# Attention by chunks with a gated MLP behind it: room for w_in from the start, ten pairs of buffers, and another order of the first batch's dense work

## The chip, the cores and the metric

The kernel runs on one core of a Trainium2 chip. The metric is the device time in microseconds of one execution. A core has five engines with a queue each: PE (matmul), DVE (vector), ACT (activation and copies), POOL (GpSimd) and SP, which here issues all DMAs. Each engine works through its queue in order, and an instruction that waits holds back everything behind it.

## The reference

```python
for t in range(S):                     # B, H, S, D = 4, 8, 768, 40
    y[:, :, t] = einsum('bhd,bhde->bhe', rt, state)
    Sa = einsum('bhde,bhe->bhd', state, at)
    state = state * wt - outer(Sa, bt) + outer(vt, kt)
x = y as (B, S, 320)
h = gelu(x @ w_in)                     # 320 x 1024, tanh form
u, v = halves of h
v_n = (v - mean) / sqrt(var + 1e-6) * g_ln
v_s = einsum('ts,bsd->btd', w_sg, v_n) + b_sg
out = x + (u * v_s) @ w_out            # 512 x 320
```

## The kernel before

The recurrence is worked in 12 chunks of 64 steps, for the four batches (b = 0 to 3) side by side. For each chunk there are gates (`gate_w` to `gate_k`, scans of the decays and products of keys, ahead of the chain by two to three chunks), the inverse of a triangular matrix (row steps on DVE, then the long list of steps on POOL that write `tg` and `x`, then `inv_back` with DVE transposes into `x1z` and `xt`, then `inv_g` and `inv_x` on PE) and the chain `chain1` to `chain5`, in which the state passes from chunk to chunk. `chain5` writes `yt`, and SP stores it to `xd`, the input of the dense part.

The order of all instructions is written out by hand: every step has a position in a plan, 28 positions to a chunk and 14 to a half chunk (c, hf), and `half` sorts the steps of a half by position. Each engine keeps this program order. Position 252 is the start of chunk 9, 336 that of the last half, in which only the y of the last chunk is left.

The dense part (`Mlp`) works in pairs of float32r numbers, a high half h and a low half l, that stand for one float32. `split64` brings one 128 x 256 tile of w_in (or a part of w_out) into such a pair in six steps: `load` (SP, into one of three buffers `stg`), `size` (ACT), `fields` and `scale` (DVE), `parts` (ACT), `low` (three steps on DVE or POOL). Twelve tiles make up w_in. `DEC` gives each tile's position and its engine for `low` (0 DVE, 1 POOL), and `DSTEP` the distance of the six steps from it. Before, `PIN` is 266.02, the position at which the gates' pool has been closed: only there `open_in` allots wih, wil, the stage buffers and the temporaries, so no tile is loaded earlier. `PX` loads half of the first batch's x (4 DMAs), `PS` splits it, `PL` loads the other half, and `PF` issues the three pieces v0, v1 and v2 while the attention part still runs.

The pieces are v0 to v5 (8 products of 512 columns, gelu, normalization, and the pair vh, vl), u0 to u7 (8 products of 384 columns, gelu), s0 to s7 (18 products with w_sg, then gate and the pair gy, gx) and o0 to o5 (products with w_out, add of x, store). s wants all six v of its batch. o0 to o2 want s0 to s3, o3 to o5 want s4 to s7. `product` issues a piece's products, and the steps behind it follow at once, one or two pieces later. `FIRSTS` is the order of the first pieces, `SEQ` that of one batch's s and o with the next batch's v and u between them. At places of this order stand the splits of w_sg (`SGS`, engine by `SGE`: V DVE, G POOL) and the six steps of the eight tiles of w_out (`OUTS`, `OSTEP`, `OUTE`).

Of the kernel before, what the change touches and what calls it, by code (L numbers as in the profile page):

```python
# [69 lines left out]
FILLERS = ("v0", "v1", "v2")  # L70
FIRSTS = ("v0", "v1", "v2", "u1", "u0", "u2", "v3", "u3", "v4", "v5", "u4", "u5", "u6", "u7")
SEQ = ("s1", "s2", "s0", "s3", "s4", "v0", "s5", "v1", "o0", "o1", "o2", "s6", "s7", "v2", "u0", "v3", "u1", "v4",
    "v5", "o3", "o5", "o4", "u2", "u3", "u4", "u5", "u7", "u6")
XS = 0
REST = 8
# [57 lines left out]
def attention(tc, a, xd, flag, keep, ps, mlp=None):  # L133
# [4 lines left out]
    with ExitStack() as ctx:  # L138
# [9 lines left out]
        ring_a, ring_a_end = pool("at_ring_a", "left")  # L148
        gt, gt_right = pool("at_gate", "right")
# [464 lines left out]
class Mlp:  # L614
# [3 lines left out]
    def __init__(self, tc, ps, xd, w_in, w2, g_ln, wst, b_sg, w_out, out):  # L618
        self.tc, self.ps, self.xd, self.out = tc, ps, xd, out
        self.w_in, self.w2, self.g_ln, self.wst, self.b_sg, self.w_out = w_in, w2, g_ln, wst, b_sg, w_out  # L620
        self.V, self.A, self.G, self.T, self.Q = engines(tc)
        self.ctx = ExitStack()
        self.vn, self.us, self.gs = {}, {}, {}
        self.n, self.todo, self.plan = 0, [], None
# [4 lines left out]
    def open_in(self):  # L629

        self.ps.grow()
        self.sb = p = self.pool("mlp_in", "right")
        self.wih, self.wil = (p.tile([128, 3, DF], F32R, name=n) for n in ("wih", "wil"))
        self.mhalf = p.tile([128, 1], F32, name="mhalf")
        self.G.memset(self.mhalf, -0.5)

    def open_x(self):
        p = self.pool("mlp_x", "right")
        self.xts = [p.tile([128, 3, S], F32, name=f"xt{i}") for i in range(2)]
        self.xh = p.tile([128, 3, S], F32R, name="xh")  # L640
        self.xl = p.tile([128, 2, S], F32R, name="xl")

    def open_v(self):
        self.pv = self.pool("mlp_v", "right")

    def open_rest(self):
        self.pr = p = self.pool("mlp_rest", "left")
        self.wsh, self.wsl = (p.tile([128, 6, S], F32R, name=n) for n in ("wsh", "wsl"))
        self.woh = p.tile([128, 4, DM + 64], F32R, name="woh")
        self.wol = p.tile([128, 4, DM - 64], F32R, name="wol")  # L650
        self.bt = p.tile([128, S], F32, name="bt")
        self.gl = p.tile([128, 4], F32, name="gl")

# [77 lines left out]
    def weights_rest(self):  # L731
        def part_sg(k, c):
            n = S // 2
# [22 lines left out]
        def rest():  # L756
            for t in (self.gl, self.bt):
                self.V.tensor_scalar(out=t, in0=t, scalar1=0.5, scalar2=None, op0=ALU.mult)
# [4 lines left out]
        wo = [part_out(k, c) for c in range(2) for k in range(4)]  # L763
        return [load_rest, rest], loads, parts, wo

    def load_x(self, b, n):

        Q, t = self.Q, self.xts[b % 2]
        c = slice(384 * n, 384 * n + 384)
        for k in range(2):  # L770
            Q.dma_start(out=t[:, k, c], in_=self.xd[b, 128 * k:128 * k + 128, c])
        for k in range(2):
            Q.dma_start(out=t[64 * k:64 * k + 64, 2, c], in_=self.xd[b, 256:320, c])

# [23 lines left out]
    def in_v(self, b, tt):  # L798
# [8 lines left out]
        bs = sb.tile([128, 6], F32, name="bs", bufs=3)  # L807

# [16 lines left out]
    def in_u(self, b, f, n):  # L825
# [5 lines left out]
        u = self.us[b, f, n] = self.pr.tile([128, 384], F32, name="u", bufs=8)  # L831
        self.product([(o, *x) for x in ops], *self.gelu2(o, 384, u))

    def sgu(self, b, f, n):
# [6 lines left out]
        o = self.ps("sg")[:, 0:384]  # L841
        g = sb.tile([128, 384], F32, name="g", bufs=2)

        def one():
            V.scalar_tensor_tensor(out=g, in0=o, scalar=self.gl[:, f:f + 1], in1=self.bt[:, c], op0=ALU.mult, op1=ALU.add)
            V.tensor_tensor(out=g, in0=g, in1=self.us.pop((b, f, n)), op=ALU.mult)
# [7 lines left out]
    def outp(self, b, m, n):  # L854
# [4 lines left out]
        o = self.ps("op")[:, 0:384]  # L859
        ops = []  # L860
# [9 lines left out]
        def one():  # L870
            x = self.xts[b % 2]
            y = sb.tile([128, 384], F32, name="y", bufs=2)[0:r]
            if m < 2:
                V.tensor_tensor(out=y, in0=o, in1=x[:, m, c], op=ALU.add)
            else:
                V.tensor_tensor(out=y, in0=o[64:128], in1=x[64:128, m, c], op=ALU.add)
# [5 lines left out]
    def side(self, c, hf):  # L882
# [5 lines left out]
        if self.plan is None:  # L888
            self.plan = plan
            at(PIN, self.open_in)  # L890
# [11 lines left out]
            at(PS, lambda: self.split_x(0, 0))  # L902
            at(PV, self.open_v)
            at(PL, lambda: self.load_x(0, 1))
            for k, p in enumerate(PF):
                at(p, lambda k=k: self.in_v(0, k))
# [3 lines left out]

    def run(self, ahead, verdict=None):

        if not ahead:
            self.open_in()
# [5 lines left out]
            for n in range(2):  # L920
                self.load_x(0, n)
            self.split_x(0, 0)
        self.open_rest()
        names = [x for x in FIRSTS if not ahead or x not in FILLERS]
        seq, jobs = [(x, 0) for x in names], [(XS, lambda: self.split_x(0, 1))]
        for b in range(B):
            if b + 1 < B:
                p = len(seq)
                for n in range(2):
                    jobs += [(p, lambda b=b, n=n: self.load_x(b + 1, n)), (p + 1, lambda b=b, n=n: self.split_x(b + 1, n))]  # L930
            seq += [(x, b + (x[0] in "uv")) for x in SEQ if x[0] in "so" or b + 1 < B]
            if b == 1 and verdict:
                jobs.append((p + 6, lambda: self.later((8, 9, verdict()))))
# [10 lines left out]
        for i, (x, b) in enumerate(seq):  # L944
            while jobs and jobs[0][0] <= i:
                jobs.pop(0)[1]()
            k = int(x[1])
            if x[0] == "u":
                self.in_u(b, k % 4, k // 4)
            elif x[0] == "v":  # L950
                self.in_v(b, k)
            elif x[0] == "s":
                self.sgu(b, k % 4, k // 4)
            else:
                self.outp(b, k % 3, k // 3)
# [114 lines left out]
```

## Time and profile before

| | us |
|---|---|
| median of 3 runs (lowest to highest) | 674.15 (673.51 to 678.35) |
| profiled execution, span from first to last instruction | 676.4 |
| PE busy | 582.4 |
| DVE busy | 525.3 |
| ACT busy | 391.3 |
| POOL busy | 367.2 |

The profiled execution's own time is not given beside its span; the span is 2.2 us above the median of the runs. Times in the rows are microseconds from the start of the span. A row of the timeline holds start, duration, engine, line, operation, target and sources with their shapes, count, and in brackets how long the engine stood idle ahead of it and for whom. PEclk 1.00 is 2.4 GHz, 0.50 is 1.2 GHz. All instructions have the same line because a helper records them, so they are told apart by their tiles.

### The profile page before, as it was taken

The numbers are of one execution on the slowest core, as the hardware profiler recorded it, in microseconds if no ns is written. First come the engines' busy times: TensorE is split into PE (matmuls) and PEld (weight loads), VectorE is DVE, ScalarE is ACT, GpSimd is POOL, SyncE is SP. The second block draws the span as 40 slices with busy tenths as digits, with TensorE's granted clock in tenths as the row PEclk, the third lists the DMA queues.
The fourth block names the chain that finished last, engine by engine and source line by source line (L and its number), as shares of the span: only waits on it lengthen the run. The fifth ranks groups of instructions, "written<-read, shape, count | busy, mean of one in ns | idle before, by whom it ended". The sixth has DMA issues, their size and how long they took to land.

```text
span 676.4 us, 22453 instructions
## 1 busy us (share of the span) xinstructions
PE 582.4 (86%) x8950; PEld 525.1 (78%) x8950; DVE 525.3 (78%) x1204; ACT 391.3 (58%) x1106; POOL 367.2 (54%) x813
## 2 busy tenths in 40 slices
PE   6336899989999899998978798697599999999996
PEld 5235787878888788887967687586599999999995
DVE  7898879889889898898777547888769668757742
ACT  5445767979779788797755644552345234434410
POOL 5216786877877878778781423544532334232321
PEclk9555589999999999999978678888699999999998
DMA  6731234343433443433334322340103001100001
GB/s 220 215 98 44 77 99 112 100 108 109 126 110 109 111 116 106 109 90 99 92 99 118 96 71 69 102 136 13 32 1 100 1 30 51 49 31 1 29 24 41
DMA packets 57617, 56.54 MB, mean 84 GB/s; under 512 B 35936, under 2 KB 47456, under 8 KB 57504
## 3 DMA queue, kind: packets, MB, share of 16 engines
q1 hardware_dynamic: 57504, 55.02, 28.4%
q8 instruction: 72, 1.18, 0.7%
q14 instruction: 41, 0.34, 0.2%
HBM read 47.14 MB, written 7.86 MB: 81 GB/s over the span
## 4 chain that ended last, share of the span: by engine, by line
PE 45%; DVE 25%; ACT 17%; issue 7%; DMA 3%; POOL 1%; SPq 1%; DVEq 0%; POOLq 0%; ACTq 0%
PE sg L119 12%; PE hu L119 7%; PE hv L119 6%; PE op L119 6%; PE ab L119 4%; ACT xt L119 3%; DVE sc L119 3%; PE sp L119 3%; DVE x L119 2%; PE pq L119 2%; DVE at L119 2%; ACT nts L119 2%; PE ru L119 2%; ACT gs L119 2%; PE yp L119 2%
## 5 line engine op out<-in xcount | busy, mean ns | idle before, releaser
L119 POOL TENSOR_TENSOR tg<-x,n 128x126 f32<-128x126 f32 (+21 forms) x318 | 116.9, 368 | 51.7 <-DVE x L119 14.2
L119 POOL TENSOR_TENSOR x<-x,tg 128x126 f32<-128x126 f32 (+21 forms) x318 | 122.2, 384 | 24.9
L119 POOL TENSOR_TENSOR gx<-g,gy 128x384 fp32r<-128x384 f32 x32 | 33.0, 1034 | 89.7 <-ACT gy L119 89.7
L119 PE MATMUL sg<-wsh,vh 128*128 128x384 f32 x192 | 66.9, 349 | 5.4 <-ACT vh L119 5.0
L119 PE MATMUL ab<-at,kb 64*64 64x64 f32 x1536 | 44.5, 246 | 29.9 <-POOL kb L119 14.2
L119 ACT ACTIVATE nts<-ab 32x256 f32<-32x256 f32 x192 | 62.2, 324 | 13.6 <-DVE at L119 11.2
L119 PE MATMUL sg<-wsh,vl 128*128 128x384 f32 x192 | 66.7, 348 | 1.5 <-POOL vl L119 1.5
L119 PE MATMUL sg<-wsl,vh 128*128 128x384 f32 x192 | 66.5, 346 | 0.7 <-POOL wsl L119 0.7
L119 PEld LDWEIGHTS ab<-at,kb 64*64 64x64 f32 x1536 | 35.2, 153 | 39.6 <-POOL kb L119 15.8
L119 PE MATMUL pq<-rt,vut 128*128 128x128 f32 x384 | 60.6, 306 | 3.4 <-ACT vut L119 2.9
L119 PEld LDWEIGHTS pq<-rt,vut 128*128 128x128 f32 x384 | 52.3, 211 | 6.6 <-ACT vut L119 3.1
L119 ACT CAST gy<-g 128x384 fp32r<-128x384 f32 x32 | 16.4, 513 | 70.6 <-DVE g L119 70.6
L119 PE MATMUL yp<-pqs,kbt 128*64 128x64 f32 x768 | 49.0, 233 | 4.2 <-DVE pqs L119 3.1
L119 ACT COPY vs<-sc 64x160 f32<-64x160 f32 x88 | 28.3, 321 | 37.0 <-DVE sc L119 36.1
L119 ACT CAST vh<-v 128x512 fp32r<-128x512 f32 x24 | 14.9, 621 | 55.5 <-DVE v L119 55.5
L119 PEld LDWEIGHTS yp<-pqs,kbt 128*64 128x64 f32 x768 | 39.9, 145 | 7.3 <-DVE pqs L119 3.5
L119 PE MATMUL yp<-rt,s 80*40 80x64 f32 x704 | 45.5, 230 | 0.0
L119 DVE SCALAR_TENSOR_TENSOR g<-sg,gl,bt 128x384 f32<-128x384 f32 x32 | 19.7, 616 | 30.3 <-PE sg L119 29.3
L119 POOL TENSOR_TENSOR vl<-v,vh 128x512 fp32r<-128x512 f32 x24 | 31.3, 1303 | 21.5 <-ACT vh L119 21.4
L119 PEld LDWEIGHTS sg<-wsh,vh 128*128 128x128 f32 x192 | 37.7, 196 | 6.6 <-ACT vh L119 5.7
L119 POOL TENSOR_TENSOR rs<-rs,mhalf 128x1 f32<-128x1 f32 x24 | 13.4, 560 | 52.6 <-DVE rs L119 51.6
L119 PE MATMUL op<-gy,woh 128*128 128x384 f32 x96 | 33.1, 352 | 10.1 <-POOL woh L119 6.2
(140 smaller groups left out, 1679.2 us busy)
## 6 DMA issues: line engine op xcount, KB each, us to landing
main<-main SPq DMA_DIRECT2D x88, 160.8 KB
vu<-vs SPq DMA_DIRECT2D x24, 160.0 KB
vs<-vb SPq DMA_DIRECT2D x24, 160.0 KB
rt<-rt SPq DMA_DIRECT2D x48, 80.0 KB
vut<-vt SPq DMA_DIRECT2D x24, 160.0 KB
xd<-yt SPq DMA_DIRECT2D x96, 40.0 KB
xt<-xd SPq DMA_DIRECT2D x16, 192.0 KB
out<-y SPq DMA_DIRECT2D x16, 192.0 KB
```

What stands on the lines that cost most here:

```text
L119: return self.tc.keep_in_program_order(f(*a, **k))
```

## The change

`open_in` is called as the attention part begins, so w_in, its stage buffers and temporaries have room while the gates run; PIN keeps only the growth of the PSUM ring. `DEC` and `DSTEP` are new numbers, and a tile's first step may stand ahead of PIN. The first half of x is loaded at 266.05. `FILL` gives five pieces of the first batch a position in the plan (the split x0, then v0, v1, v2, u0), and `AFTER` a position to each step behind them, where before these followed piece by piece. The splits of x are pieces of their own in the order, with the loads `XL` = 3 places ahead; x stands in four tiles of half a batch. vh and vl come from a list of ten pairs (`VRING`) in place of rings of eight, and the u tiles go by name. `SEQ0` is the order of the first batch, with the split of the next batch's x0 ahead of v4, and u0 of the next batch and s6 between o0 and o2. `SGE` puts four of the twelve w_sg splits on DVE, where it was six. The scratch for dynamic DMAs is set to 1024.

```diff
 PIN = 266.02
-DSTEP = ((-9.0, -1.0, 0.0, 0.7, 1.4, 2.4), (-9.0, -1.0, 0.0, 0.7, 1.4, 3.0))
-DEC = ((275.0, 0), (280.0, 0), (285.0, 0), (289.66, 0), (295.0, 1), (300.0, 0), (305.0, 1), (310.0, 1), (315.0, 1),
-    (320.0, 1), (325.0, 1), (330.0, 1))
-PX = 294.02
-PS = 318.92
-PV = 313.14
+DSTEP = ((-11.56, -2.45, 0.0, 1.2, 2.6, 3.84), (-12.47, -0.81, 0.0, 0.36, 2.6, 4.5))
+DEC = ((272.17, 0), (276.63, 0), (282.72, 0), (287.41, 0), (291.65, 1), (297.75, 1), (300.46, 1), (306.04, 0),
+    (311.03, 1), (313.66, 1), (321.04, 1), (327.61, 1))
+PX = 266.05
+PV = 294.03
 PL = 335.9
-PF = (338.0, 342.0, 345.87)
-FIRSTS = ("v0", "v1", "v2", "u1", "u0", "u2", "v3", "u3", "v4", "v5", "u4", "u5", "u6", "u7")
-SEQ = ("s1", "s2", "s0", "s3", "s4", "v0", "s5", "v1", "o0", "o1", "o2", "s6", "s7", "v2", ...
-SGS = (5, 3, 5, 6, 7, 8, 8, 11, 10, 11, 12, 11)
-OUTS = (10, 11, 12, 13, 14, 15, 16, 17)
-OSTEP = (-2, 0, 0, 0, 0, 1)
-SGE = "GVGVGVGVVVGG"
+FILL = (("x0", 0, 322.97), ("v0", 0, 330.19), ("v1", 0, 347.66), ("v2", 0, 347.67), ("u0", 0, 349.9))
+AFTER = {"v": (0.5, 0.6, 1.5, 1.64, 2.04, 2.83, 2.93, 4.23, 5.31), "u": (0.5, 1.09, 1.99, 2.04), "x": ()}
+EARLY = 5
+VRING = 10
+SEQ = ("x0", "s1", "x1", "s2", "s0", "s3", "s4", "v0", "s5", "v1", "o0", "o1", "o2", "s6", "s7", "v2", ...
+SEQ0 = (("x0", 0), ("v0", 0), ("x1", 0), ("u0", 0), ("v2", 0), ("u1", 0), ("u2", 0), ("v1", 0), ("u3", 0), ("v3",
+    0), ("x0", 1), ("v4", 0), ("v5", 0), ("u5", 0), ("u4", 0), ("u6", 0), ("u7", 0), ("s1", 0), ("x1", 1), ("s2",
+    0), ("s0", 0), ("s3", 0), ("v0", 1), ("v1", 1), ("s5", 0), ("s4", 0), ("o0", 0), ("u0", 1), ("o1", 0), ("s6",
+    0), ("o2", 0), ("s7", 0), ("v3", 1), ("v2", 1), ...
+XL = 3
+SGS = (3, 5, 6, 8, 6, 10, 10, 13, 12, 13, 14, 13)
+OUTS = (11, 12, 13, 14, 15, 16, 17, 18)
+OSTEP = (-3, 0, 0, 0, 0, 1)
+SGE = "GVGVGVGGGVGG"
...
         ring_a, ring_a_end = pool("at_ring_a", "left")
+        if mlp:
+            mlp.open_in()
         gt, gt_right = pool("at_gate", "right")
...
+    def pairs(self, p, lo, hi):
+        return [[p.tile([128, HF], F32R, name=f"v{x}{i}") for x in "hl"] for i in range(lo, hi)]
...
+        if self.hold is not None:
+            self.hold += [f for _, _, f in sorted(steps, key=lambda x: x[:2])]
+            return
         self.later(*steps)
...
-            at(PIN, self.open_in)
+            at(PIN, self.ps.grow)
...
-                    at(max(PIN + 0.1, DEC[k][0] + d), lambda k=k, i=i: step(k, i))
+                    at(DEC[k][0] + d, lambda k=k, i=i: step(k, i))
...
+            for x, b, p in FILL:
+                at(p, lambda x=x, b=b: self.early(x, b))
+                for d in AFTER[x[0]]:
+                    at(p + d, lambda x=x, b=b: self.held[x, b].pop(0)())
...
+    def early(self, x, b):
+        self.held[x, b] = self.hold = []
+        self.piece(x, b)
+        self.hold = None
...
-    nc = bacc.Bacc("TRN2", target_bir_lowering=False, num_devices=1)
+    nc = bacc.Bacc("TRN2", target_bir_lowering=False, num_devices=1, dynamic_dma_scratch_size=1024)
```

## Rows read from the trace of the kernel before

**Rows 1.** The page: busy time of PE and DVE with their share and count, the span in 40 slices for PE (tenths), and the DMA queue of the data.

```profile
PE 582.4 (86%) x8950; PEld 525.1 (78%) x8950; DVE 525.3 (78%) x1204; ACT 391.3 (58%) x1106; POOL 367.2 (54%) x813
PE   6336899989999899998978798697599999999996
q1 hardware_dynamic: 57504, 55.02, 28.4%
```

**Rows 2.** The table by stretches: from and to, length, then busy time (and count) of PE, PEld, DVE, ACT and POOL, the granted clock, the DMA share and GB/s.

```profile
345.00:358.60 13.60, 13.28 (x173) 12.21 (x170) 10.46 (x29) 6.89 (x20) 9.26 (x24) 0.50 0.27 78
375.70:396.20 20.50, 18.24 (x204) 16.58 (x204) 11.29 (x31) 11.40 (x33) 9.07 (x13) 0.50 0.28 75
411.40:429.00 17.60, 17.60 (x89) 16.59 (x89) 13.26 (x27) 9.65 (x21) 6.70 (x7) 0.95 0.37 106
429.00:442.00 13.00, 6.52 (x23) 4.79 (x23) 10.17 (x21) 6.18 (x14) 6.48 (x7) 0.68 0.42 124
463.40:483.50 20.10, 9.28 (x33) 6.46 (x33) 16.73 (x42) 7.59 (x23) 9.90 (x20) 0.78 0.04 11
478.10:488.40 10.30, 5.95 (x18) 5.55 (x19) 8.39 (x19) 3.60 (x8) 5.48 (x8) 0.50 0.11 38
516.25:574.90 58.65, 58.65 (x324) 56.09 (x323) 43.14 (x90) 24.23 (x50) 19.48 (x20) 1.00 0.13 39
```

**Rows 3.** The timeline of DVE, the transposes into x1z of the last three chunks and the row steps ahead of the last one, and of POOL, the end of the last inverse.

```profile
307.01 1.10 DVE L119 STREAM_TRANSPOSE x1z<-x 128x512 f32<-128x512 f32 x1
330.38 1.10 DVE L119 STREAM_TRANSPOSE x1z<-x 128x512 f32<-128x512 f32 x1
359.61 1.41 DVE L119 SCALAR_TENSOR_TENSOR x<-x,n 128x15 f32<-128x15 f32 x3
361.05 1.08 DVE L119 STREAM_TRANSPOSE x1z<-x 128x512 f32<-128x512 f32 x1
...
355.67 0.28 POOL L119 TENSOR_TENSOR x<-x,tg 128x45 f32<-128x45 f32 x1
```

**Rows 4.** The timeline of SP's queue from 355 to 365, of ACT at the wait for the tile, of PE at its two long waits, and the piece of the chain of waits that is the tile's transfer (start, duration, what).

```profile
355.69 1.87 SPq L119 DMA_DIRECT2D xd<-yt  x4
...
360.14 3.18 SPq L119 DMA_DIRECT2D xt<-xd  x4
364.00 1.06 SPq L119 DMA_DIRECT2D stg<-w_in  x2
...
364.00 4.76 DMA stg<-w_in
...
368.79 0.43 ACT L119 ACTIVATE sc<-stg 128x256 f32<-128x256 f32 x1 [5.02 <-DMA stg<-w_in]
...
343.93 0.30 PE L119 MATMUL ru<-rhsb,xt 64*64 64x40 f32 x2 [3.68 <-ACT xt L119]
377.79 0.43 PE L119 MATMUL ru<-rhsb,xt 64*64 64x40 f32 x2 [4.59 <-ACT xt L119]
```

**Rows 5.** The timeline of PE at the last yp of the attention part.

```profile
409.62 0.34 PE L119 MATMUL yp<-pqs,kbt 128*64 128x64 f32 x4 [2.75 <-DVE pqs L119]
```

**Rows 6.** The timeline of PE at its waits in the dense start, that of POOL at the last tile of w_out, and two pieces of the chain of waits, one u and one s.

```profile
435.06 0.69 PE L119 MATMUL sg<-wsh,vh 128*128 128x384 f32 x1 [3.80 <-ACT vh L119]
...
466.56 0.45 PE L119 MATMUL op<-gy,woh 128*128 128x384 f32 x1 [3.12 <-ACT gy L119]
...
476.20 0.44 PE L119 MATMUL op<-gy,woh 128*128 128x384 f32 x1 [1.63 <-POOL woh L119]
...
483.03 0.69 PE L119 MATMUL op<-gy,woh 128*128 128x384 f32 x1 [4.01 <-POOL woh L119]
...
482.66 0.32 POOL L119 TENSOR_TENSOR woh<-stg,lt 128x64 fp32r<-128x64 f32 x1
...
418.51 1.42 PE hu L119 x8
...
533.68 3.12 PE sg L119 x18
```

**Rows 7.** Groups of DVE's instructions from 397 to 676, shapes kept apart: names, shapes, count, busy time, mean ns of one, and idle time ahead of them.

```profile
L119 DVE BATCH_NORM_STATS2 bs<-v 128x6 f32<-128x512 f32 x24 | 16.7, 695 | 0.8
L119 DVE SCALAR_TENSOR_TENSOR v<-q,hv 128x512 f32<-128x512 f32 x24 | 16.4, 683 | 2.3 <-ACT q L119 2.3
L119 DVE SCALAR_TENSOR_TENSOR q<-p,hv 128x512 f32<-128x512 f32 x24 | 16.4, 683 | 14.4 <-ACT p L119 14.4
L119 DVE TENSOR_SCALAR v<-v,mv,rs 128x512 f32<-128x512 f32 x24 | 15.8, 659 | 1.0 <-POOL rs L119 0.7
L119 DVE TENSOR_TENSOR xl<-xt,xh 128x384 fp32r<-128x384 f32 x14 | 9.5, 718 | 1.7 <-ACT xh L119 1.6
...
L119 DVE TENSOR_TENSOR wsl<-ws,wsh 128x384 fp32r<-128x384 f32 x6 | 4.1, 702 | 1.4 <-ACT wsh L119 1.4
```

**Rows 8.** The timeline of DVE at two splits of w_sg, and that of POOL at a vl and at the first of the three low steps of a tile of w_in.

```profile
421.46 0.55 DVE L119 TENSOR_TENSOR wsl<-ws,wsh 128x384 fp32r<-128x384 f32 x1
...
428.34 1.45 DVE L119 TENSOR_TENSOR wsl<-ws,wsh 128x384 fp32r<-128x384 f32 x1 [1.10 <-ACT wsh L119]
...
428.08 1.29 POOL L119 TENSOR_TENSOR vl<-v,vh 128x512 fp32r<-128x512 f32 x1
...
377.09 0.72 POOL L119 TENSOR_TENSOR lt<-lt,sc 128x256 f32<-128x256 f32 x1 [1.16 <-ACT wih L119]
```

More of the change, by code (lines that the diff above doesn't have):

```diff
@@ L622, in __init__ @@
         self.ctx = ExitStack()
-        self.vn, self.us, self.gs = {}, {}, {}
-        self.n, self.todo, self.plan = 0, [], None
+        self.vn, self.us, self.gs, self.xin, self.left, self.outs = {}, {}, {}, {}, [8] * B, {}
+        self.ready = set()
+        self.n, self.todo, self.plan, self.hold, self.held = 0, [], None, None, {}
     def pool(self, nm, side):
@@ L638, in open_x, with xtile @@
         p = self.pool("mlp_x", "right")
-        self.xts = [p.tile([128, 3, S], F32, name=f"xt{i}") for i in range(2)]
+        self.xts = {(0, 0): self.xtile(p, 0, 0)}
         self.xh = p.tile([128, 3, S], F32R, name="xh")
         self.xl = p.tile([128, 2, S], F32R, name="xl")
+    def xtile(self, p, b, n):
+        return p.tile([128, 3, S // 2], F32, name=f"xt{b}{n}")
     def open_v(self):
-        self.pv = self.pool("mlp_v", "right")
+        self.pv = p = self.pool("mlp_v", "right")
+        self.xts.update({x: self.xtile(p, *x) for x in ((1, 0), (0, 1))})
+        self.free = self.pairs(p, 0, EARLY)
+        self.ut = {(f, 0): p.tile([128, 384], F32, name=f"u{f}") for f in range(4)}
+    def pairs(self, p, lo, hi):
+        return [[p.tile([128, HF], F32R, name=f"v{x}{i}") for x in "hl"] for i in range(lo, hi)]
     def open_rest(self):
@@ L652, in open_rest @@
         self.gl = p.tile([128, 4], F32, name="gl")
+        self.xts[1, 1] = self.xtile(p, 1, 1)
+        self.free += self.pairs(p, EARLY, VRING)
+        self.ut.update({(f, 1): p.tile([128, 384], F32, name=f"u{4 + f}") for f in range(4)})
     def tmp(self, nm, n, dt=F32):
@@ L841, in sgu @@
         o = self.ps("sg")[:, 0:384]
+        assert self.ready >= {"gl", *((k, n) for k in range(6))}
+        u = self.ut[f, n] = self.us.pop((b, f, n))
+        self.left[b] -= 1
+        if not self.left[b]:
+            self.free += [self.vn.pop((b, t)) for t in range(6)]
         g = sb.tile([128, 384], F32, name="g", bufs=2)
@@ L859, in outp @@
         o = self.ps("op")[:, 0:384]
+        self.outs[b, n] = self.outs.get((b, n), 0) + 1
+        assert all(("wo", i) in self.ready for i in range(8))
         ops = []
@@ L909, in side, with piece @@
         return [(p - lo, f) for p, f in self.plan if lo <= p < hi]
+    def early(self, x, b):
+        self.held[x, b] = self.hold = []
+        self.piece(x, b)
+        self.hold = None
+    def piece(self, x, b):
+        k = int(x[1:])
+        if x[0] == "u":
+            self.in_u(b, k % 4, k // 4)
+        elif x[0] == "v":
+            self.in_v(b, k)
+        elif x[0] == "s":
+            self.sgu(b, k % 4, k // 4)
+        elif x[0] == "o":
+            self.outp(b, k % 3, k // 3)
+        else:
+            self.split_x(b, k)
     def run(self, ahead, verdict=None):
+        done = [(x, b) for x, b, _ in FILL] if ahead else []
+        seq, jobs = [], []
         if not ahead:
+            self.ps.grow()
             self.open_in()
@@ L919, in run @@
             self.open_v()
-            for n in range(2):
-                self.load_x(0, n)
-            self.split_x(0, 0)
         self.open_rest()
-        names = [x for x in FIRSTS if not ahead or x not in FILLERS]
-        seq, jobs = [(x, 0) for x in names], [(XS, lambda: self.split_x(0, 1))]
         for b in range(B):
[L927 to L933, printed above, removed]
+            seq += [(x, b + (x[0] in "uvx")) for x in SEQ] if b else list(SEQ0)
+        seq = [x for x in seq if x[1] < B and x not in done]
+        for i, (x, b) in enumerate(seq):
+            if x[0] == "x" and (b or not ahead) and not (ahead and (x, b) == ("x0", 1) and PX1):
+                jobs.append((max(0, i - XL), lambda b=b, n=int(x[1]): self.load_x(b, n)))
+            if verdict and (x, b) == ("s7", 1):
+                jobs.append((i, lambda: self.later((8, 9, verdict()))))
         rest, loads, parts, wo = self.weights_rest()
```

60 lines of the change are left out of this document (28 added, 32 removed), and 2 rows, old and new, of the table SEQ0.

## Prediction, made before the changed kernel was run

> **What bounds the kernel now.** I read the page first: PE is busy 86% of the span and DVE 78% [rows 1], but the slices show that the two take turns. Behind slice 29 PE is full; ahead of it are slices with 5 to 8 tenths, so the second view is the table by stretches, which also tells the granted clock: 1.00 in some, 0.50 in others [rows 2]. A batch of dense work in the steady part, 516.25 to 574.9, holds PE for all of its 58.65 us at full clock, with DVE at 43.14: PE alone sets the time there, and the order of the steady batches (SEQ) differs only in where a split of x stands. The last stretch is left as it is, too. What can move lies in two stretches ahead.
>
> The first is the end of the attention part. DVE's transposes into x1z mark positions 28 apart in the plan, 241.18, 269.18 and 297.18: 307.01, 330.38 and 361.05 us [rows 3]. So one chunk took 23.37 us, the next one 30.67, and from 297.18 to the last yp of the attention part, which ends at 411.4, 52.8 positions took 50.4 us. At 23.37/28 = 0.835 us a position they would take 44.1.
>
> The second is the start of the dense work, 411.4 to 483.5. The PE table by stretches shows two holes: 6.52 busy of 13.0 us and 9.28 of 20.1, with DVE at 10.17 and 16.73 [rows 2]. The timeline of PE says for whom it waited: for vh of the last rows of v, then for gy, then for the low halves of w_out [rows 6].
>
> **The part of the change in the attention's end.** The room for w_in from the start lets the first tile be split from 272.17 instead of 275, and the load be queued from 260.6 instead of 266.1. The number of tiles and their work don't change: the twelve stand 5.0 positions apart before and 5.04 after. So the room by itself takes nothing off the path. What it gives is a place for the loads. The one load that came late shows it [rows 4]: SP was held by the four stores of yt at 355.69, then issued rt and vut, the four of x (3.18 us) and vs, and got to the tile of w_in at 364.00; ACT stood for it until 368.79, for 5.02 us, with the copies of the chain (vs, vut, gs, xt) behind it in its queue, and PE stood for xt 4.59 us. This is tile 6, with its load at position 296. After, that load stands at 287.99, ahead of those stores, and the loads of x leave this place for 266.05. Next in line is tile 7, at 294.48: behind stores, rt and vut SP is free at about 360.1, tile 7 also wants the buffer of tile 4 (on POOL, whose inverse ends at 355.95 [rows 3], so perhaps at 361), and with the 4.76 us from issue to landing [rows 4] it is there at 364.9 to 365.8, where ACT came for its tile at 363.8. So 1.1 to 2.0 of the 5.02 us stay: -3.5, bounds 0 and -5.0.
>
> Behind this hole PE had the low clock from 375.7 to 396.2 with 18.24 us busy; at full clock this work is 9.1 [rows 2]. Bounds 0 and -9.1. The other PE wait of this size, 3.68 us at 343.93 [rows 4], also stands right ahead of a stretch at the low clock, 345 to 358.6 [rows 2]; a hole of 1 to 2 us may or may not do it. I take about half of what the pace allows on top: the two terms together -7, next to the 50.4 - 44.1 = 6.3 of the undisturbed pace and far from the -14.1 at which both go.
>
> Ahead of 297.18 the gain has a floor: POOL's steps of the last inverse end at 355.95 [rows 3], and nothing in the change starts them earlier; with the three row steps on DVE (1.41, [rows 3]) the transpose can't be ahead of 357.4, so 0 to -3.7; I take -1.5.
>
> At the end, the last yp stood 2.75 us for the mask product on DVE, which came behind two tiles of v [rows 5]. After, v1 and v2 are issued behind the last pq (347.66 against 346.76) and u0 behind the yp ahead of it, so PE has work there: 0 to -2.75, I take -2. u0's own 1.4 us on PE is moved from behind the end to ahead of it, so it costs this part what it gives the next one: 0.
>
> This part: -7 - 1.5 - 2 = -10.5, bounds 0 and -20.6.
>
> **The part in the dense start.** Until s1 PE waits for DVE, so DVE's work counts [rows 7]. Ahead of it come the split of x0 of the next batch (2 x 0.718 = 1.4, and a third step of half the partitions, about 2 in all) and what v1 and v2 leave undone at the end of attention: one tile costs 0.683 + 0.683 + 0.695 + 0.659 = 2.7 and small ones, so up to 6 us, where before about one tile's work of the three came behind 411.4. Away go the two steps of u0, shorter than those of a v. That is +2 to +4 us on DVE, while PE has one product less to cover it. Against that, DVE was busy only 13.26 of 17.6 us until 429.0 [rows 2], so most of it fits in there. I take +1 with bounds -3 and +4 for the first hole.
>
> Two of the twelve splits of w_sg go from DVE to POOL: -2 x 0.702 on DVE if nothing else happens. The trace speaks against counting that: the split took DVE 0.55 us at 421.46, and 1.45 at 428.34, while POOL did vl [rows 8]. If each moved split holds up other DVE work for the 0.9 us seen here, the term is +0.4, if none does, -1.4; I take 0. The Trainium skill (SBUF — State Buffer, Who interferes with whom) speaks against the move: a DVE instruction with two SBUF inputs contends with a GpSimd instruction that reads SBUF, so by its rule alone the term would be at the upper end, and with no such rule at the lower one; these rows agree with the rule.
>
> The second hole is 20.1 - 9.28 = 10.8 us. Its waits: 3.12 for gy at o0, and 1.63 and 4.01 inside o2 for woh [rows 6], and smaller ones. The last low half of w_out POOL wrote at 482.98 [rows 6]. Before, the eight tiles of w_out are issued until one place ahead of o0, and o0, o1, o2 follow each other. After, they end two places ahead of o0, and u0 of the next batch (1.42) and s6 (3.12, by a u and an s of [rows 6]) stand between o0 and o2, as does the second split of x further ahead. So PE has 4.5 us of other work while the last tiles come; of the 5.64 us at o2 I take 5, of the 3.12 at o0 1.5 (DVE has the 2 us of the x0 split behind it by then). PE had the low clock from 478.1 to 488.4 with 5.95 us busy [rows 2]: up to half of that, -3.0, more, of which I take 1.5. Together -8, bounds 0 and -13.8.
>
> This part: +1 + 0 - 8 = -7, bounds +4.4 and -18.2.
>
> **What costs nothing.** The ten pairs of vh and vl: in the steady part no wait of PE names them, since PE is full, so neither gain nor cost. The x tiles in four halves: the same bytes and DMAs. The smaller scratch for dynamic DMAs: all data queues of the page are of the hardware kind [rows 1], so nothing uses it.
>
> **The sum.** 676.4 - 10.5 - 7 = 658.9 us of span. The span of the profiled execution is 2.2 us above the median of the runs, so 656.7; I say 656.5 us.
>
> **The rivals.** First, only the dense start gains: tile 7 or another comes late, ACT stops as before and the clock falls as before. For it speaks that three buffers hold twelve tiles and now every load from tile 3 on stands 0.2 to 3.8 positions ahead of the release that it needs, where before it stood 3 or more behind it. 674.15 - 7 = 667. Second, only the attention's end gains, because DVE, not the order, sets the dense start (10.17 of 13.0 and 16.73 of 20.1 us busy in the holes): 674.15 - 10.5 = 663.7. Third, it doesn't do what it says: the weights still come at the same pace, the chain is as slow, and the dense start stops at vh longer than it saves at woh: 674, give or take 5.
>
> Fourth, slower: the same buffers make SP wait. A load at 298.56 waits for tile 5's low half at 302.25, one at 301.19 for tile 6's at 304.96, both on POOL (three steps of about 0.72, 2.2 us [rows 8]), and SP's stores of yt, rt and vu queue up behind. The lead left to tile 9 is 312.85 - 304.96 = 7.9 positions less 2.2 us, so 4.4 to 5.7 us against 4.76 to landing. It decides from the point where a tile lands later than ACT asks for it by more than the hole which PE can cover. One more such stop costs 5.0 + 9.1 = 14.1 us: without the gain at the attention's end 674.15 + 14.1 - 7 = 681, and 688 if the dense start gives nothing. Against it: the leads are only just short, and a slower chain leaves the loads more time.
>
> **How the numbers follow.** Both parts gain, 0.50, with 641 to 663 as the range of this case; only attention 0.13; only the dense start 0.12; nothing 0.13; slower 0.12. 1% of 674 is 6.7 us, about what a measurement of this kernel can tell from no change. Below 667.4: the first two and most of the third, less a few of the first, 0.70. Within 1%: 0.18. Slower: 0.12. The range goes from 641, where most terms come near their bounds (33 of the 39 us that all bounds together would give), to 676, which leaves out the slower case and the upper end of the third rival.
>
> **What would show it.** In the changed profile: no wait of ACT for w_in above 2 us; x1z of the last chunk at 357 to 361; the end of yp at about 401; PE's stretches at the low clock ahead of that shorter by 10 us; between the last yp and s1 a hole as large as before; no wait for woh above 2 us at o2; a batch in the steady part at 58.5 us still. It is wrong if ACT stops again for a tile, if PE's holes at s1 grow by more than 4 us, or if the steady part loses its full PE.

## The result and the profile after

| | before | after |
|---|---|---|
| median (lowest to highest), runs | 674.89 (673.51 to 678.35), 4 | 655.61 (655.06 to 657.6), 4 |
| profiled execution, its span | 678.35, 676.4 | 655.47, 653.7 |

The ratio is 0.9729, 95% interval 0.9679 to 0.9779: 19.3 us less, where 18 were forecast. The profiled execution of before was the longest of its runs, so the two traces stand 22.6 us apart, 3.3 more than the medians. The working below goes from trace to trace and keeps that in mind.

The page of after: PE's busy time with its share and count, then its tenths in 40 slices (before: [rows 1]).

```profile
PE 574.4 (88%) x8950; PEld 517.5 (79%) x8950; DVE 527.8 (81%) x1202; ACT 389.8 (60%) x1106; POOL 372.3 (57%) x815
PE   6435799999899998999989898796999999999996
```

Between the first five slices and the last one only two of after have under 8 tenths, the 26th and the 28th (7 and 6); before it was five, the 21st, 23rd, 26th, 28th and 29th (7, 7, 6, 7 and 5). The table by stretches of after, to set beside [rows 2]: the two stretches at the low clock ahead of the last yp, the time from there to the first sg, the hole behind it, and o0 to the end of o2 with u0 and s6 between them.

```profile
340.70:361.20 20.50, 20.24 (x244) 18.53 (x244) 17.09 (x42) 10.55 (x33) 15.61 (x34) 0.50 0.45 122
371.50:378.30 6.80, 6.54 (x76) 5.92 (x78) 4.01 (x12) 4.55 (x14) 4.13 (x6) 0.50 0.35 101
397.80:416.80 19.00, 17.12 (x80) 15.32 (x81) 17.20 (x35) 11.54 (x26) 8.54 (x10) 0.91 0.50 149
416.80:431.10 14.30, 9.49 (x38) 7.73 (x37) 11.67 (x24) 7.53 (x18) 7.31 (x8) 0.76 0.46 139
452.20:465.80 13.60, 12.92 (x60) 11.24 (x61) 11.00 (x28) 4.81 (x15) 7.10 (x16) 0.87 0.02 6
```

The timeline of after: two of the transposes into x1z, of positions 241.18 and 297.18 [rows 3], PE's waits for xt [rows 4], the end of the last yp [rows 5], and the waits in the dense start [rows 6].

```profile
305.07 1.09 DVE L125 STREAM_TRANSPOSE x1z<-x 128x512 f32<-128x512 f32 x1
...
357.49 1.07 DVE L125 STREAM_TRANSPOSE x1z<-x 128x512 f32<-128x512 f32 x1
...
340.79 0.43 PE L125 MATMUL ru<-rhsb,xt 64*64 64x40 f32 x2 [2.52 <-ACT xt L125]
371.16 0.31 PE L125 MATMUL ru<-rhsb,xt 64*64 64x40 f32 x2 [1.72 <-ACT xt L125]
...
397.50 0.28 PE L125 MATMUL yp<-rt,s 80*40 80x64 f32 x4
...
421.66 0.44 PE L125 MATMUL sg<-wsh,vh 128*128 128x384 f32 x1 [2.27 <-ACT vh L125]
...
452.23 0.45 PE L125 MATMUL op<-gy,woh 128*128 128x384 f32 x1 [3.98 <-ACT gy L125]
```

Three pieces hold the difference. Up to the transpose at position 241.18, after is 1.9 us ahead (305.07 against 307.01); nothing of the change is near there, and the low clock early on is shorter by 6.8 us in this one execution, so I take it for chance: over the traces of all fourteen kernels this transpose starts anywhere from 303.90 to 309.65. From there to the end of the last yp it took 92.7 us in place of 104.4: -11.7. From the last yp to the end of the span it took 256.0 in place of 265.0: -9.0. (u0's 1.4 us of PE work changed sides; put back, the two are -13.1 and -7.6.) PE's wait for woh inside o2 is gone, that for gy at o0 has grown from 3.12 to 3.98. From the end of o2 on, 188.0 us are left in place of 192.7, the difference being the u0 and s6 (4.5 us) that now stand ahead of it: the steady part is the same.

The attention part can be cut at two events of the chain: the transpose at position 297.18, and the product ru behind PE's second long wait for xt in [rows 4], simply "the ru" from here on. From 241.18 to that transpose it took 54.0 us before and 52.4 after (-1.6); from the transpose to the ru 16.7 and 13.7 (-3.1); from the ru to the last yp 33.6 and 26.6 (-7.0).

The waits view from 318 to the last yp (who waited for what: us in total, times, longest), first of before, then of after, shows what else is different:

```profile
DVE sc L119 <- ACT sc L119: 13.6, 6, 3.6
ACT lt L119 <- DVE lt L119: 11.6, 9, 2.8
PE ru L119 <- ACT xt L119: 8.7, 4, 4.6
ACT sc L119 <- DMA stg<-w_in: 5.0, 1, 5.0
```

```profile
PE ru L125 <- ACT xt L125: 4.7, 4, 2.5
ACT lt L125 <- DVE lt L125: 2.2, 3, 1.3
DVE sc L125 <- ACT sc L125: 0.6, 1, 0.6
```

ACT no longer stands for a tile of w_in at all. There is another difference, of which the prediction did not speak: `size` (sc) and `parts` (lt, wih) are on ACT, `fields` and `scale` on DVE. Before, these two engines stood 26.2 us for each other's steps of a tile (the two rows here and 1.0 of DVE for ACT's lt), after 7.4 (with 4.6 of that last kind). How much time hangs on these waits, and how much on the late tile, the sums do not tell; that takes the experiments.

### The profile page after: what moved, and what is told of

The parts are those of the page before. It is cut to its first block, busy times and chain, and to the rows that moved or that the text cites. A ratio compares the mean times of both kernels' runs of the same rounds, so it can differ in the third digit from the quotient of the medians.

```text
span 653.7 us, 22448 instructions
## 1 busy us (share of the span) xinstructions
PE 574.4 (88%) x8950; PEld 517.5 (79%) x8950; DVE 527.8 (81%) x1202; ACT 389.8 (60%) x1106; POOL 372.3 (57%) x815
## 3 DMA queue, kind: packets, MB, share of 16 engines
q8 instruction: 72, 1.18, 0.8%
## 4 chain that ended last, share of the span: by engine, by line
PE 47%; DVE 23%; ACT 19%; issue 7%; DMA 3%; POOL 1%; SPq 1%; DVEq 0%; POOLq 0%; ACTq 0%
PE sg L125 12%; PE op L125 6%; PE hv L125 5%; PE ab L125 5%; PE hu L125 4%; PE sp L125 3%; ACT nts L125 3%; PE pq L125 3%; PE yp L125 3%; ACT xt L125 2%; DVE x L125 2%; PE ru L125 2%; DVE sc L125 2%; ACT junk L125 2%; DVE at L125 2%
## 5 line engine op out<-in xcount | busy, mean ns | idle before, releaser
L125 ACT ACTIVATE nts<-ab 32x256 f32<-32x256 f32 x192 | 62.0, 323 | 13.7 <-DVE at L125 11.3
L125 PE MATMUL pq<-rt,vut 128*128 128x128 f32 x384 | 58.8, 301 | 0.4 <-DVE yt L125 0.2
L125 PEld LDWEIGHTS pq<-rt,vut 128*128 128x128 f32 x384 | 50.5, 205 | 3.4 <-DVE yt L125 0.6
L125 PE MATMUL yp<-rt,s 80*40 80x64 f32 x704 | 44.0, 225 | 0.0
L125 DVE TENSOR_TENSOR at<-ab,mask 64x256 f32<-64x256 f32 x96 | 35.8, 409 | 5.7 <-PE ab L125 5.4
```

The source lines that it names most:

```text
L125: return self.tc.keep_in_program_order(f(*a, **k))
```

## The experiments

Each kernel is the changed one with an edit. The ratios are to the kernel before on the same chip, whose median was 672.75 us for `attention_only`, `dense_only`, `x_late` and `old_tiles`, 673.31 for `step_old`, `x_behind`, `old_fill` and `o_together`, and 675.54 for the last four; the changed kernel's ratio is 0.9729.

### The two parts, each alone

`attention_only` has the old order and places in the dense part, `dense_only` the old positions and distances of the tiles, the old loads of x and pieces in the attention part.

```diff
 attention_only: SEQ0, SGE, OUTS, OSTEP, SGS as before
 dense_only:     DEC, DSTEP, PX, PV, x0 and v0 to v2 as before, u0 behind
```

> The attention part of the changed kernel (tiles, x loads, v0, v1, v2 and u0 inside it) with the order of the first batch's dense work, the w_sg split engines and the places of the w_out steps as before. My theory: the two parts add up, and the attention's end is worth about 11 us of the 19: 663 to 666, with the last yp at 398 and the waits for woh at o2 back (6 us or more). Rival, the dense order alone carries the gain because the earlier end of attention is lost again waiting for DVE: 670 to 675.

> The tiles, the x loads and the places of x0, v0, v1 and v2 as before, u0 behind the attention part again; the changed dense order, engines of the w_sg splits and places of the w_out steps. My theory: 665 to 668, the last yp at 409 to 412, and the two holes of the dense start together 8 us shorter than before. Rival, DVE and not the order sets the dense start: 672 or more.

`attention_only` took 667.16 us, ratio 0.9906 (0.9869 to 0.9943); `dense_only` 664.31, 0.9892 (0.9833 to 0.9951). Both parts gain; 6.3 and 7.3 us together are 13.6, and the whole change gives 18.3 (2.71% of 674.89). By traces, `attention_only` took 93.8 us from position 241.18 to the last yp (after 92.7) and 266.2 from there on (before 265.0); the wait for woh stands in it as before (first line). Behind its last yp there is a new loss, too: with u0's 1.4 us no longer in it, the first hole took 21.4 us where before it took 17.6, and PE stands there for the split of x (the other two lines):

```profile
474.12 0.69 PE L123 MATMUL op<-gy,woh 128*128 128x384 f32 x1 [4.20 <-POOL woh L123]
...
405.28 0.92 PE L123 MATMUL hv<-wih,xh 128*128 128x512 f32 x2 [0.73 <-ACT xh L123]
...
408.24 0.79 PE L123 MATMUL hv<-wih,xh 128*128 128x512 f32 x1 [2.05 <-DVE xh L123]
```

`dense_only` took 257.9 us from the last yp on, 7.1 less than before, which is about its whole gain by the medians. In its trace the attention part is 6.4 us shorter, too (98.0), against the "409 to 412" of the expectation. This execution took 661.57 us, 2.7 less than its median, and that of before 3.5 more than its own, so the times leave room for only a part of these 6.4. Where they lie is this (`dense_only`, then one line of before):

```profile
357.91 1.05 DVE L125 STREAM_TRANSPOSE x1z<-x 128x512 f32<-128x512 f32 x1
...
361.78 0.45 ACT L125 ACTIVATE sc<-stg 128x256 f32<-128x256 f32 x1 [1.18 <-DMA stg<-w_in]
...
364.34 1.16 PE L125 MATMUL pq<-rt,vut 128*128 128x128 f32 x8 [0.19 <-ACT vut L125]
...
371.79 0.43 PE L125 MATMUL ru<-rhsb,xt 64*64 64x40 f32 x2 [4.59 <-ACT xt L125]
```

```profile
370.34 1.16 PE L119 MATMUL pq<-rt,vut 128*128 128x128 f32 x8 [2.94 <-ACT vut L119]
```

SP issued the loads of x at 315 to 325, though their position is again 294.02; why they went ahead here and not in before was not tried. ACT's stop at tile 6 fell from 5.02 to 1.18, with the tiles' positions and distances still those of before. PE's wait is the same 4.59 us as in [rows 4], but the ru comes 13.9 us behind the transpose where before it came 16.7: the stop had put off all of ACT's copies ahead of xt, and it shows at an earlier product, pq, where PE waited 2.94 us for ACT's vut before and 0.19 here. By the time of xt PE and ACT were late alike. The other 3.5 us lie behind the ru, where the low clock held for 10.9 us less than before.

### Where the loads of x stand

```diff
 x_late:   -PX = 266.05   +PX = 294.02
 x_behind: the same, and DVE clears a column of the tile of x ahead of the loads
```

> The changed kernel with the first half of x loaded at 294.02 instead of 266.05, so that these four DMAs stand ahead of tile 7 in SP's queue again. My theory of SP's queue: tile 7 lands 3.2 us later, ACT stops for it by 3 to 5 us, PE gets the low clock behind it: 660 to 670. Rival, the distances of the tiles' steps and not the queue made the gain at the attention's end: 654.5 to 657.

> The changed kernel with the four DMAs of the first half of x held to position 294.02 by a write of one column on DVE (in x_late they went ahead all the same), so that they stand behind the stores of yt and ahead of a tile of w_in in SP's queue, as before the change. SP's queue theory: that tile lands 3.2 us later, ACT stops 1 to 4 us for it: 657 to 664. Theory of the distances: the longer lead of the tiles takes it up, 654.5 to 657.

`x_late` took 658.64 us (0.9791, 0.9739 to 0.9844) and tells nothing of its question, since SP issued the loads just as early:

```profile
316.70 0.37 SPq L125 DMA_DIRECT2D xt<-xd  x1
...
337.89 0.47 SPq L125 DMA_DIRECT2D xt<-xd  x1
```

The column that DVE clears holds them at their place in `x_behind`, which took 658.73 (0.9773, 0.971 to 0.9837): four loads at 358.04, and ACT stops 1.37 us at the next tile, tile 7. That is inside the 1.1 to 2.0 of the prediction, but for another reason: the prediction had worked it out with these four loads gone. Without them (after, last line) SP is at tile 7 by 357.44, and nothing stops.

```profile
358.04 2.25 SPq L125 DMA_DIRECT2D xt<-xd  x4
...
360.39 0.53 SPq L125 DMA_DIRECT2D stg<-w_in  x1
...
364.57 0.44 ACT L125 ACTIVATE sc<-stg 128x256 f32<-128x256 f32 x1 [1.37 <-DMA stg<-w_in]
...
357.44 0.38 SPq L125 DMA_DIRECT2D stg<-w_in  x1
```

To the last yp it took 93.3 us, 0.6 more than after. The intervals of both runs overlap the changed kernel's.

### The positions and the distances of the tiles' steps

```diff
 old_tiles: DEC and DSTEP as before, first steps not ahead of PIN + 0.1
 step_old:  DSTEP as before
 load_old:  -11.56 and -12.47 to -9.0 (the loads alone)
 inner_old: -2.45, 0, 1.2, 2.6, 3.84 and -0.81, 0, 0.36, 2.6, 4.5
            to -1.0, 0, 0.7, 1.4, 2.4 (3.0) (the five steps behind the load)
```

> The changed kernel with the positions and step distances of the twelve tiles as before (first step not ahead of 266.12). My theory of SP's queue: without the x loads ahead of it tile 6 lands at about 365 and ACT stops for 1 to 2 us instead of 5; with closer steps ACT and DVE wait more for each other: 657 to 662. Rival, the tiles' positions carry all of the attention part's gain: 666 or more.

> The changed kernel with the distances of a tile's six steps as before (DSTEP), its positions (DEC) and all else as changed. After the first four runs PE's 4.59 us wait for xt stood without a late tile in dense_only (there ACT stopped 1.2 us for DMA), while ACT waited for DVE's and DVE for ACT's steps of the tiles. Theory of the distances: those waits come back (DVE for ACT's sc above 5 us, ACT for DVE's lt above 5), PE waits 4 us for xt again: 660 to 666. My first theory, SP's queue alone: 654.5 to 657.5.

> The changed kernel with one thing put back: the load of each tile of w_in stands 9.0 positions ahead of its fields step, where the change has 11.56 and 12.47. Everything else, the order of ACT and DVE too, stays as changed. Theory of the late load (the prediction's step: ACT stands for a tile's transfer with the chain's copies behind it): ACT's idle time for the DMA comes back with 3 to 5 us ahead of the last yp, PE's wait for xt grows to 4 us and more, the last yp ends 3 to 7 us later than the 397.8 of the changed kernel, and the time is 659 to 663. Theory of the steps' distances (ACT and DVE wait for each other's tile steps): ACT's idle time for the DMA may come back, but the idle time of DVE for sc and of ACT for lt stays under 4 us, the last yp ends by 400, and the time is 655 to 658.

> The changed kernel with the other part of the distances put back: size, fields, scale, parts and low of a tile of w_in stand at -1.0, 0, 0.7, 1.4 and 2.4 (3.0 on POOL) as before, while the loads stay 11.56 and 12.47 ahead as changed. Theory of the steps' distances: DVE's idle time for sc and ACT's for lt come back with 8 to 15 us each ahead of the last yp, PE waits 4 to 5 us for xt twice without ACT standing for a DMA, the last yp ends at 405 to 411, and the time is 662 to 667. Theory of the late load: within 1.5 us of the changed kernel, 655 to 658.

The times: `old_tiles` 667.24 us (0.9909, 0.9874 to 0.9944), `step_old` 664.97 (0.985, 0.9782 to 0.9917), `load_old` 659.99 (0.9778, 0.9738 to 0.9819), `inner_old` 665.08 (0.9849, 0.9808 to 0.989). The table has, in us: ACT's stops for a tile of w_in, with the tile's number; the waits of DVE and ACT for each other's sc and lt from 318 to the last yp; the time at the low clock between the transpose at 297.18 and the last yp; the three pieces from 241.18 to the transpose at 297.18, to the ru and to the last yp, with their sum; and how far the profiled execution stood from its kernel's median.

| | stops (tile) | DVE and ACT | low clock | to 297.18 | to the ru | to last yp | sum | profiled less median |
|---|---|---|---|---|---|---|---|---|
| before | 5.0 (6) | 26.2 | 22.0 | 54.0 | 16.7 | 33.6 | 104.4 | +3.5 |
| old_tiles | 5.0 (0), 0.5 (6) | 25.2 | 20.5 | 58.5 | 13.9 | 31.8 | 104.1 | +3.2 |
| step_old | 3.6 (1) | 22.5 | 14.4 | 55.9 | 17.4 | 27.5 | 100.8 | +3.5 |
| inner_old | none | 21.8 | 10.7 | 54.8 | 17.4 | 27.2 | 99.4 | +0.5 |
| dense_only | 1.2 (6) | 24.4 | 11.1 | 54.0 | 13.9 | 30.1 | 98.0 | -2.7 |
| load_old | 5.0 (1) | 11.3 | 6.8 | 54.7 | 13.7 | 26.5 | 94.9 | -0.1 |
| old_fill | none | 6.7 | 8.0 | 52.4 | 13.7 | 28.2 | 94.3 | -0.1 |
| x_behind | 1.4 (7) | 9.2 | 10.2 | 52.5 | 13.7 | 27.2 | 93.3 | -0.6 |
| after | none | 7.4 | 10.5 | 52.4 | 13.7 | 26.6 | 92.7 | -0.1 |

The last column bids care, but the pieces repeat better than whole executions do: the four traces with the attention part of after (after, `o_together`, `u_ahead`, `eight_six`) have 92.6 to 93.0 us from 241.18 to the last yp, with 17.1 to 27.3 us of low clock between 318 and the last yp.

The price of tile 6's stop stands in the column "to the ru". The two kernels with old positions and old distances whose stop at tile 6 is short, `dense_only` and `old_tiles`, both have 13.9 us there, 2.9 less than before, with PE's wait for xt at 4.59 in all three and its wait for vut at 0.19 in these two. The lines of `old_tiles`:

```profile
365.98 1.05 DVE L125 STREAM_TRANSPOSE x1z<-x 128x512 f32<-128x512 f32 x1
...
369.20 0.46 ACT L125 ACTIVATE sc<-stg 128x256 f32<-128x256 f32 x1 [0.54 <-DMA stg<-w_in]
...
379.86 0.43 PE L125 MATMUL ru<-rhsb,xt 64*64 64x40 f32 x2 [4.59 <-ACT xt L125]
```

`load_old` does not put this stop back. Its one stop is at tile 1, 32 us earlier, and all that it costs lies ahead of 297.18: 2.2 us, 3.3 by the ratios, whose intervals overlap the changed kernel's. In `inner_old` ACT never waits for a transfer, and 6.7 us of the gain are gone, 8.1 by the ratios: 2.4 ahead of 297.18, 3.7 from there to the ru, 0.6 behind it. But that is what the old distances cost at the new positions. At the old positions they cost next to nothing up to the ru (13.9 against 13.7), although `dense_only` and `old_tiles` have 24 to 25 us of the two engines' waits for each other, so the sum of these waits is no measure of the time either. ACT, then PE of `load_old`:

```profile
336.89 0.43 ACT L125 ACTIVATE sc<-stg 128x256 f32<-128x256 f32 x1 [4.95 <-DMA stg<-w_in]
...
340.07 0.66 ACT L125 COPY vs<-sc 64x160 f32<-64x160 f32 x2 [2.14 <-DVE sc L125]
...
346.69 0.30 PE L125 MATMUL ru<-rhsb,xt 64*64 64x40 f32 x2 [1.14 <-ACT xt L125]
```

Behind the stop ACT's next step of the chain, vs, still waited 2.14 us for DVE's sc, so much of the stop lay beside a wait that was there anyhow (in after vs waits 3.10 there, at 334.19). Now DVE, ACT and PE of `inner_old` at the first of the two long waits for xt, and then ACT at the same place in after; the last two lines of `inner_old` are the transpose and the ru:

```profile
341.03 0.43 DVE L125 TENSOR_TENSOR lt<-lt,sc 128x256 f32<-128x256 f32 x1 [1.93 <-ACT lt L125]
...
344.62 0.42 ACT L125 ACTIVATE lt<-lt 128x256 f32<-128x256 int32 x1 [1.93 <-DVE lt L125]
...
345.28 1.17 ACT L125 COPY xt<-xp 32x512 f32<-32x512 f32 x2
...
345.90 0.43 PE L125 MATMUL ru<-rhsb,xt 64*64 64x40 f32 x2 [5.27 <-ACT xt L125]
...
362.25 1.07 DVE L125 STREAM_TRANSPOSE x1z<-x 128x512 f32<-128x512 f32 x1
...
379.67 0.43 PE L125 MATMUL ru<-rhsb,xt 64*64 64x40 f32 x2 [5.11 <-ACT xt L125]
```

```profile
338.66 0.41 ACT L125 ACTIVATE lt<-lt 128x256 f32<-128x256 int32 x1
...
340.16 1.17 ACT L125 COPY xt<-xp 32x512 f32<-32x512 f32 x2
```

DVE stands 1.93 us for one tile's lt from ACT. ACT then stands as long for the next tile's lt from DVE, and the copy xt that PE needs is queued behind this step: PE waits 5.27 us, in after 2.52. Of these 2.75 us 1.93 are ACT's wait, the rest is about the two tile steps between it and xt. In after DVE stands for ACT at this place too (2.15 us at 339.10), but with `parts` 2.6 positions behind `fields` in place of 1.4 no second tile's lt stands in ACT's queue ahead of xt, and the circle isn't closed. In before PE's wait at this place was 3.68 [rows 4].

### The pieces inside the attention part

```diff
 old_fill: x0 at 318.92, v0, v1, v2 at 338.0, 342.0, 345.87, steps behind
           them piece by piece, u0 behind the attention part
```

> The changed kernel with x0, v0, v1 and v2 at the places of before (318.92, 338, 342, 345.87), the steps behind them piece by piece as before, and u0 behind the attention part. My forecast gave their move 2 us: the last yp waits 2.5 to 3 us for the mask product again, 656.5 to 659. Rival, v1 and v2 at the end of attention only push their DVE work into the dense start: 652 to 655.5.

660.94 us, 0.9814 (0.9753 to 0.9875), more than expected. The wait of [rows 5] is back (first line; the other two are the transpose at 297.18 and the ru):

```profile
399.78 0.34 PE L125 MATMUL yp<-pqs,kbt 128*64 128x64 f32 x4 [2.76 <-DVE pqs L125]
...
359.51 1.08 DVE L125 STREAM_TRANSPOSE x1z<-x 128x512 f32<-128x512 f32 x1
...
373.20 0.43 PE L125 MATMUL ru<-rhsb,xt 64*64 64x40 f32 x2 [2.63 <-ACT xt L125]
```

To the last yp it took 94.3 us, without u0's products, so 1.6 + 1.4 = 3.0 us more, and 257.7 behind it (after 256.0, without u0). With u0 behind the end and the pieces as before, its attention part differs from that of `dense_only` mainly in the tiles' positions and distances (both issue the loads of x early): 94.3 against 98.0 us. So, by one trace of each, new positions and distances together are worth 3.7 us there, 1.6 ahead of 297.18, 0.2 up to the ru and 1.9 behind it.

### The order of the dense start

```diff
 o_together: -o0, u0, o1, s6, o2, s7   +o0, o1, o2, u0, s6, s7
 u_ahead:    -o0, u0, o1               +u0, o0, o1
```

> The changed kernel with o0, o1, o2 one behind the other again, and u0 of the next batch and s6 behind them. My theory: PE waits for the last tiles of w_out inside o2 again, 4 to 6 us, 658.5 to 662. Rival, the tiles' steps two places earlier are enough and the order is free: 654.5 to 657.

> The changed kernel with u0 of the second batch ahead of o0, where it stands behind it. In the changed kernel PE stands 3.98 us at the first product of o0 for gy, and u0's products are 1.4 us of work that needs nothing of it. If the wait at o0 is set by the chain of gate steps on DVE and ACT alone, PE's wait falls to 2.5 and the time by 1 to 1.5 us: 654 to 655. Rival: u0's own gelu steps get ahead of the last gate steps in the queues of ACT and DVE, gy comes later by as much, and the time stays or grows by up to 1 us: 655.5 to 657.

`o_together` took 662.65 us, 0.9823 (0.9756 to 0.9889): the wait for woh is back, and 261.1 us stand behind the last yp, 5.1 more than in after. The eight traces with this order of after have 255.6 to 258.4 us there, so the order is worth 2.7 to 5.5.

```profile
467.85 0.45 PE L125 MATMUL op<-gy,woh 128*128 128x384 f32 x1 [3.31 <-POOL woh L125]
```

`u_ahead` took 659.05, 0.9768 (0.9727 to 0.981): no gain.

```profile
456.98 0.44 PE L125 MATMUL op<-gy,woh 128*128 128x384 f32 x1 [2.59 <-ACT gy L125]
...
460.74 0.69 PE L125 MATMUL op<-gy,woh 128*128 128x384 f32 x1 [0.81 <-ACT gy L125]
```

The first wait fell by 1.39, just u0's products, but PE then waited 0.81 at a later gy and had 6.8 us of low clock behind the hole where after had 3.4; from the last yp to the end of o2 it took 68.2 us, after 68.0. What u0 fills of the hole comes back at the next gy, and the clock of this one execution may have its part in it.

### The pairs and the splits of w_sg

```diff
 eight_six: -VRING = 10   +VRING = 8
            -SGE = "GVGVGVGGGVGG"   +SGE = "GVGVGVGVVVGG"
```

> The changed kernel with eight pairs of vh and vl in place of ten, and six of the w_sg splits on DVE in place of four. The prediction put both at nothing (-1.4 to +0.4 for the splits): 654.5 to 657.5. Theory of contention (a DVE split of 0.55 us takes 1.45 beside POOL's): up to 1.4 us faster or, with DVE's queue ahead of s1 fuller, up to 2 us slower with a longer wait of PE for wsl or vh ahead of s1. Theory that the pairs hold the next batch's v back: a wait of DVE or ACT for PE's s products ahead of the third v of batch 1, 1 to 3 us slower.

657.95 us, 0.9742 (0.97 to 0.9785), and 255.6 us behind the last yp against 256.0: nothing that the times or the traces show, for both together. No wait names a pair. The splits on DVE, with one beside POOL's vl:

```profile
411.20 0.55 DVE L125 TENSOR_TENSOR wsl<-ws,wsh 128x384 fp32r<-128x384 f32 x1
...
419.98 1.52 DVE L125 TENSOR_TENSOR wsl<-ws,wsh 128x384 fp32r<-128x384 f32 x1 [0.82 <-ACT wsh L125]
...
419.82 1.27 POOL L125 TENSOR_TENSOR vl<-v,vh 128x512 fp32r<-128x512 f32 x1
```

The Trainium skill (SBUF — State Buffer, Who interferes with whom) states that a DVE instruction with two SBUF inputs contends with a GpSimd instruction that reads SBUF. These rows agree: the split took 1.52 us in place of 0.55 and ended at 421.50, 0.41 us behind the end of vl. Two splits more or less on DVE change nothing in the time here.

## Why the prediction was right

The time (656.5 forecast, 655.61 measured) and both parts hold: attention -10.5 forecast, -11.7 in the traces; dense start -7, -9.0 in the traces, -7.6 without u0's change of sides. The traces differ by 3.3 us more than the medians, so the parts are a little smaller in the times. By steps:

- The late tile, -3.5: it holds. Up to the ru the change took off 3.1 us, and `dense_only` and `old_tiles`, which have a short stop at tile 6 and all distances as before, show 2.9 of them. The prediction's sign for it was wrong: "PE stood for xt 4.59 us" is the same 4.59 with a stop of 5.02, 1.18 and 0.54; the stop's cost stood at pq, 2.94 us for vut. Also, no tile stops ACT in after, where tile 7 was to do it for 1.1 to 2.0: its load was issued at 357.44, not at 360.1 or later.
- "So the room by itself takes nothing off the path" is wrong. `dense_only` has the room (and the new tiles of x), but the positions and the distances of before, and its stop at tile 6 is 3.8 us shorter: the loads of x no longer stood ahead of this tile's.
- The low clock behind it, -3.5: in size it fits, but it can't be put on the stop. With the same positions, distances and pieces, before took 3.5 us more than `dense_only` from the ru to the last yp, with 10.9 us more of low clock. But `old_tiles` had the low clock for as long as before (20.5 us) with a stop of only 0.54. What brings it on is open, and before's was the longest of its executions, so a part of this piece is the luck of one trace.
- Ahead of 297.18, -1.5: from 241.18 to 297.18 it took 52.4 us in place of 54.0, -1.6. That the transpose came at 357.49, beside the floor of 357.4, is luck: 1.9 us of it are the chance ahead of 241.18. Counted from there the floor is 50.4 us, and it took 52.4.
- The last yp, -2: the wait is gone, and `old_fill` brings 2.76 us of it back, with 3.0 us on the stretch with u0's work (1.6 without).
- Left out: what the new positions and distances do behind 297.18. By `dense_only` and `old_fill`, one trace each, that is 2.1 us, the 1.6 ahead of 297.18 not counted. The prediction spoke of the tiles' number and work alone. That its steps could have cost 6.7 us at the new positions, with the old distances, it didn't see (`inner_old`).
- The first hole, +1: from the last yp to the first sg 19.05 us in place of 17.59, +1.5, with u0's 1.4 no longer in it. DVE holds PE up there, as forecast, in a wait that before did not have; behind it after had 3.4 us of low clock. In four other kernels with the same wait (`x_late`, `x_behind`, `u_ahead`, `eight_six`) the clock stayed up and the hole took 17.41.

```profile
404.51 0.50 PE L125 MATMUL hv<-wih,xh 128*128 128x512 f32 x1 [1.88 <-DVE xh L125]
```

- The second hole, -8: from the first sg to the end of o2 48.9 us in place of 54.7, with 4.5 more work of PE in it, so -10.3. A part of that is the clock of this one execution, at 1.2 GHz for 10.2 us of the stretch where before had 19.2. Six kernels with the same order had 20.5 there, and took 51.7 to 52.4: -6.8 to -7.6 with the 4.5. No wait for woh stands in o2; `o_together` puts 2.7 to 5.5 on the order, as the term had 5. The 1.5 taken off o0's wait did not come, it is 0.86 longer.
- At nothing: the pairs and the two splits, as `eight_six` shows for both together. The x tiles in four halves and the scratch weren't tried alone.
- The rivals "only the dense start" and "only the attention's end" are refuted by the lengths of both parts, and by the two kernels that have one part each, though `dense_only` keeps the room; the slower one by ACT's waits, none of which is for a tile. The claim "low clock ahead of that shorter by 10 us" came to 6.8 (27.3 against 34.1, without the stretch that began 1.5 us ahead of the last yp's end).

That the parts give 13.6 us alone and 18.3 together is within the noise: the ends of their intervals (0.9869 and 0.9833) together reach 20 us. From position 241.18 to the end the traces show no such gap, 9.4 and 13.5 us alone and 20.7 together. What `attention_only` loses again in the first hole is part of why its gain is the smaller one.

## What to carry to other kernels

Price a stop by the way from an event ahead of it to the product that matters, not by the length of the wait that shows on the next engine: here PE's wait ahead of the ru was the same 4.59 us in three kernels, and in one of them the ru came 2.9 us later, which showed at a product further ahead. Nor does the sum of two engines' waits for each other tell the time: it was 24.4 and 26.2 us in two kernels of which the first took 6.4 us less in this part. When the tiles move, the distances of their steps have to move with them, each behind the point at which its input is surely there; the old distances at the new positions cost 6.7 us. When a put-back is to test one stop, look in its trace whether that stop came back, or another one. And read the place of a load from the queue that issues it, not from the program's plan.

## What the runs showed of the hardware

The granted clock differs from one execution to the next of the same kernel, and the time tends to go with it: of the runs of before beside `load_old`, the shortest, 670.46 us, had a mean clock of 0.912, and the longest, 678.83, one of 0.897.

The same wait can be followed by the low clock or not. In the first hole PE stands 1.86 to 1.88 us for xh in ten traces. In six of them (after, `old_tiles`, `step_old`, `load_old`, `inner_old`, `o_together`) 3.4 us at 1.2 GHz follow, and the hole takes 19.0 us; in four the clock stays at 2.4 GHz, and it takes 17.41. The hole of `eight_six`, to set beside the third line of the table of after (granted clock 1.00 and 0.91):

```profile
400.60:418.00 17.40, 15.53 (x81) 14.21 (x82) 16.07 (x32) 10.84 (x24) 8.26 (x9) 1.00 0.54 165
```

What the low clock costs depends on whether PE sets the time. In that hole 3.4 us of it cost 1.6. Between the transposes of 241.18 and 297.18 it held for 10.2 to 17.1 us in the eight traces with the new tiles and without a stop there, and all eight took 52.4 to 52.5 us.
